# A fused attention and feed-forward kernel: another written-out order of its TensorE groups and loads, and other constants in its planner

## The chip, the core and the metric

One core of a Trainium2 chip. The metric is the device time of one execution in microseconds (us); six executions of the kernel before are at hand. Five engines work side by side, each on its own list of instructions, and wait for one another by semaphores: TensorE (PE, matmuls; PEld is its weight load), VectorE (DVE), ScalarE (ACT), GpSimd (POOL) and SyncE (SP), which here only issues transfers.

## The reference

Attention with a window of 128 tokens and 4 sink tokens for 4 batches of 8 heads, 768 tokens, head size 64; its output, as 3072 tokens of 512 numbers, goes through a feed-forward layer with 2048 hidden units:

```python
scores = (q @ k.T) / sqrt(64);  keep = is_sink | (0 <= rel < 128)
a = exp(scores - max) * keep;   a = a / sum(a);   x = a @ v        # per head
h = x @ w_in;   g = h / (1 + exp(-beta * h));   out = g @ w_out
```

## The kernel before, in words

The tokens are cut into 8 half-batches of 384 tokens ("blocks" 0 to 7, `hb` in the code); each has 4 units of two heads. For a block the kernel loads q, k and v in fp32 (`load`, L613), casts them to bf16 (`cast`, L659), transposes q and k, computes scores, exponentials, masks, the product with v, normalises, transposes the result into `xT`, and then makes the hidden layer and the output. PE's work comes in groups, one letter each:

- T (L690): transposes q and k of a unit on PE, blocks 0 and 1 only; the copy out of PSUM (`qkT<-P`) is DVE's or ACT's. From block 2 on a transfer does it (`XT`, L730, issued by SP: `qkT<-q`, `qkT<-k`).
- S (L812): scores against the sinks; C and D (L764): two groups of window scores (L783), each followed by an exponential on ACT (`E<-P`) and masks on POOL or DVE (L798, L803, L809).
- A (L841): the product with v (L851, L861); then DVE's reciprocal and `onorm` (L868). `vS`, the sinks' rows of v, is copied by DVE (L686) from block v0.
- X (L873): transposes `onorm` into `xT` on PE, blocks 0 and 1; from block 2 on transfers do it (`XO`, L888, two for each block).
- h and g, or H (L899): the hidden layer for 128 hidden units, four matmuls of 128x384 (L910); h is the first two, g the other two. Then tanh on ACT (`t`, L915) and one fused operation on DVE that gives `g` (L917). There are 16 of them in a block.
- O (L925): a quarter of an output tile, four matmuls of 128x512 (L931); after four quarters the tile is copied to `osb` (three buffers, DVE or ACT) and stored by SP (L940).
- b: beta's transpose.

The weights come in sixteen chunks of 512 KB (w0 to w7 for w_in, w8 to w15 for w_out; `load_w`, L640), each cast by DVE, ACT or POOL (`cast_w`, L650) before use. Six staging buffers exist, three of which are borrowed from `g`.

What sets the order:

- `ORDER` (L24) is a string of these letters, found by a search outside of the kernel: PE's groups in the order in which they are issued.
- `PAR` (L23) holds the order of the loads: `l0` permutes the 11 loads of block 0 (indices 0 to 7 are q0, k0, q1, k1, q2, k2, q3, k3 in pairs of heads, 8 to 10 are v0 to v2); `mix` then interleaves the attention loads of blocks 1 and 2 (a) with the weight chunks (w). Both make the list LOADS (L962), which is chained, so that SP issues loads in that order.
- The planner `Graph.schedule` (L148) walks ORDER with a small model of each engine's time (`place`, L106: durations, latencies LAT and HOP, a model of the transfers in flight) and gives every other operation to an engine and a place in its list, the earliest that the model allows. An operation with several possible engines goes to the one that the model has done first. The model runs while the program is built; on the chip only the lists and their semaphore waits remain.
- `fillers` (L301): wherever the model sees PE idle before 48 us, it puts matmuls on the constant tile `ones` (L1027) into PE's list. They are issued in order like any others; nothing reads their result.

SP's list is one queue: loads, stores and transposing transfers are issued in its order, and each that must wait holds all behind it.

Of the kernel before, what the change touches and what calls it, by code (L numbers as in the profile page):

```python
# [21 lines left out]

PAR = {'MD': 1, 'XB': 2, 'l0': [0, 2, 6, 1, 3, 4, 9, 5, 7, 10, 8], 'mix': 'aawwaawawawwawwaaaawwawwawwwawaa'}  # L23
ORDER = ('TCDTSTTDCSDSCASCTADACbXXAhhhXXThghDghgDhggThgggChhgghgShDSghSghghTghgCASCAXADOXOAhhhhXOXOgOOggOOhghg'  # L24
         'hhgOOOghgghghhhghgOgOSDgSChCOghSgADODCCOODOOSAAOAOSSOCCSOSODCHHHHHHHHOHDDOHAHDCHHAHHHAAOODDOOOODCDOH'
         'SCCHHOOASSHHOHOHHHHHSHHHAACSHSOHDCCOAODDOOCCDOAOOHHSHSAOHHOHAAHHHHHHHSHOHOHOSSOCDOHDCCOHHAOOHHHHHSHH'
         'HOSOCCDOHHOHODDAHOAHAOODCCASOOOCDDHHHHHHOAOHOOSHHOOSAHHAOHHHHHOOOHHHHOOHHHHHHOOHHHHOHOOOOOHOOOOOOOOO'
         'OOOOO')
# [9 lines left out]
class Op:  # L38
    __slots__ = ("eng", "fn", "deps", "signal", "count", "waits", "sem", "vc", "dma", "seq", "end", "ns", "alts",
                 "group", "tail", "preds", "left", "succ", "at", "queue", "ring", "lag", "x", "tag", "chain")  # L40

# [5 lines left out]
class Graph:  # L47
# [3 lines left out]
    LAND = {"act": 22, "dve": 23, "gp": 58, "pe": 50, "sp": 26}  # L51
    LEAD, PAD, LATE = 1500, 2000, 90000
    BIAS, EARLY = 300, 100000
    FILL_TO = 48000
    RING, FETCH, SWITCH = 165, 900, 85
    DEPTH = 9

    def __init__(self):
        self.ops = []
        self.groups = []  # L60
        self.writers = {}
        self.readers = {}
        self.last_load = None
        self.filler = None

# [6 lines left out]
    def add(self, eng, fn, ns=0, r=(), w=(), x=(), dma=None, alts=None, queue=470, ring=64, lag=0, after=(), tag=None):  # L72


        o = Op()
        o.eng, o.fn, o.dma, o.ns, o.alts = eng, fn, dma, ns, alts or {eng: (fn, ns)}
        o.queue, o.ring, o.lag, o.x, o.tag, o.chain = queue, ring, lag, list(x), tag, None
        o.signal, o.count, o.waits, o.vc = False, 0, [], None
        o.group, o.seq = None, -1
        if eng == "pe":  # L80
            o.group = self.groups[-1]
            o.group.ops.append(o)
        deps = []
        for k in r:
            ws = self.writers.get(k)
            assert ws, k
            deps += [(p, True) for p in ws]
        for k in w:
            deps += [(p, False) for p in self.readers.get(k, ())]
            deps += [(p, False) for p in self.writers.get(k, ())]  # L90
        for bs, i in x:
            if eng != "pe":
                deps += [(p, False) for p in bs.users[i] if p.eng == "pe"][-1:]
            bs.users[i].append(o)
            bs.left[i] += 1
        deps += [(p, False) for p in after]
        o.deps = deps
        for k in r:
            self.readers.setdefault(k, []).append(o)
        for k in w:  # L100
            self.writers[k] = [o]
            self.readers[k] = []
        self.ops.append(o)
        return o

    def place(self, o, at):  # L106
        o.at = at
        if o.dma:
            self.pending = [x for x in self.pending if x[0] > at]
            issued, need = at + o.queue + 40, min(o.ring, self.RING)  # L110
            total = sum(n for _, n in self.pending)
            for f, n in self.pending:
                if total + need <= self.RING:
                    break
                issued, total = max(issued, f), total - n
            begin = issued + o.lag if o.lag else at + 1150 + o.ns
            self.dma_free = max(self.dma_free + o.ns, begin)
            self.pending.append((self.dma_free, o.ring))
            self.free[o.eng] = issued
            o.end = self.dma_free + 950 + (self.PAD if at > self.LATE else 0)  # L120
        else:
            if o.eng == "pe":
                self.n_pe += 2
                if self.n_pe >= self.fetched + 256:
                    self.fetched += 256
                    self.dma_free = max(self.dma_free, at) + self.FETCH
                rows = o.group is not None and o.group.tag in "CD"
                if rows != self.rows:
                    at = o.at = at + self.SWITCH
                    self.rows = rows  # L130
            self.free[o.eng] = at + o.ns
            o.end = at + o.ns + self.LAT[o.eng]

# [14 lines left out]
    def schedule(self, order):  # L148
# [46 lines left out]
        self.free = {e: 800.0 for e in self.ENGINES}  # L195
        self.dma_free, self.pending, self.n_pe, self.rows, self.fetched = 0.0, [], 0, False, 0
        new = []
# [39 lines left out]
        while at_pe < len(todo) or pool:  # L237
# [20 lines left out]
            for o in pool:  # L258
                opts = []
                for e, (fn, ns) in o.alts.items():  # L260
                    t = self.free[e]
                    for p in o.preds:
                        s = self.seen(p, e)
                        if s > t:
                            t = s
                    if o.dma:
                        t = max(t, self.dma_free - self.LEAD)
                    opts.append((t + ns + (self.BIAS if e == "act" and t < self.EARLY else 0), t, e))
                _, t, e = min(opts)
                by_eng.setdefault(e, []).append((t, o))  # L270
# [7 lines left out]
            if e == "pe":  # L278
                at_pe += 1
                self.fillers(t, banks, holder, new)  # L280
                for bs in fresh.values():
# [18 lines left out]

    def fillers(self, t, banks, holder, new):  # L301

        while self.free["pe"] < min(t, self.FILL_TO):
            slow = 2 if self.free["pe"] < 4900 else 1
# [3 lines left out]
            free = [j for j in range(8) if holder[j] is None and banks[j][0] <= now]  # L308
            n = min(512, int((t - now) * 2.4 / slow) // 128 * 128)
            if not free or n < 128:  # L310
# [4 lines left out]
            o.signal, o.count, o.waits, o.vc, o.chain = False, 0, [], None, None  # L315
            o.deps = [(p, True) for p in self.writers["ones"]] + [(p, False) for p in banks[j][1]]
            o.seq = len(new)
# [137 lines left out]
def _program(nc, G, sb, ps, q, k, v, w_in, w_out, beta, out):  # L455
# [274 lines left out]
    def XT(hb, i):  # L730
# [4 lines left out]
            qkT_all[:, hb % (NT // 4), i, cs[0] * 512:cs[0] * 512 + w].rearrange("p (b t) -> p b t", t=128),  # L735
            x16[n][hb % NX][:, cs[0]:cs[0] + len(cs), :, :].rearrange("p c h d -> p (c h d)")), 1500,
            r=[(n + "16", hb % NX, j, c_) for j in range(4) for c_ in cs],
            w=[("qkT", hb % (NT // 4), j, i, c_) for j in range(4) for c_ in cs], dma=f"dx{n}{hb % 2}", queue=1540, ring=999, lag=1350)

# [24 lines left out]
    def SC(u):  # L764
# [23 lines left out]
        for j, grp in enumerate(gs):  # L788
# [5 lines left out]
            for kind_, sg in (("d", 1), ("p", -1)):  # L794
                at_ = [i for i, blk in enumerate(grp) if blk[0] == kind_]
                if at_:
# [5 lines left out]
                    if UNITS[u][0] < PAR.get('MD', 2):  # L802
                        alts["dve"] = (lambda e, d=d, mk=mk: e.tensor_tensor(d, d, mk, ALU.mult),  # L803
                                       70 + 256 * len(at_) / 1.9)
                    any_of(alts, r=[("E", z, j), ("maskT", int(kind_ == "p"))], w=[(kind_, z, j)])
            if grp[0][0] == "s":
                d = E[z][:, s0:s0 + 2, :, :]
                mask = maskS[:, :, :].unsqueeze(2).to_broadcast([128, 2, 2, 128])
                fn = lambda e, d=d, mask=mask: e.tensor_tensor(d, d, mask, ALU.mult)  # L809
                any_of({"gp": (fn, 1150), "dve": (fn, 335)}, r=[("E", z, j), "maskS"], w=[("s", z, j)])  # L810

# [29 lines left out]
    def AV(u):  # L841
# [5 lines left out]
        for m, ps in enumerate(parts(u)):  # L847
# [8 lines left out]
            for hh in range(2):  # L856
                o0 = (2 * m + hh) * (D + 1)
                for n, (kind_, j, i, kb) in enumerate(ps):
                    vz = (hb if kb >= NK * half else hb - 1) % NV
                    add("pe", lambda e, o0=o0, hh=hh, i=i, kb=kb, vz=vz, a=(n == 0 and not far), o=(n == len(ps) - 1):  # L860
                        e.matmul(A()[:, o0:o0 + D + 1], E[z][:, i, hh, :], vaug[vz][:, kb % NK, 2 * hp + hh, :],  # L861
                                 start=a, stop=o, skip_group_check=True), 39,
                        r=[(kind_, z, j), ("v", vz, kb % NK)], x=[(bs, 0)])
# [24 lines left out]
    def XO(u):  # L888
# [5 lines left out]
            r=[("on", on), ("on", on + 1)], w=[("xT", hp, tl), ("xT", hp + 1, tl)], dma=f"dy{on}", queue=1260,  # L894
            ring=60, lag=700)

# [28 lines left out]
    def OQ(T_, t, j, a=0, b=NOUT):  # L925
# [9 lines left out]
        if j == 3:  # L935
            z = os_i[0] % NOS
            os_i[0] += 1
            any_of(copies(osb[z][:, a:b], lambda: P[:, bk[0], a:b], {"dve": dve_ns(b - a), "act": act_ns(b - a)}, 0.5), w=[("osb", z)],
                   x=[(bk, 0)])
            add("sp", lambda e: e.dma_start(out_t[NK * hb + t][:, a:b], osb[z][:, a:b]), 640 * (b - a) // NOUT, r=[("osb", z)],  # L940
                dma=f"do{z}", queue=370, ring=8)
# [83 lines left out]
    for x, y in zip(LOADS, LOADS[1:]):  # L1025
        loads[y].chain = loads[x]
    G.filler = lambda j, n: lambda e: e.matmul(  # L1027
        P[:, j, 0:n].rearrange("p (a b) -> p a b", b=128), ones[:, :],
        ones[:, :].unsqueeze(1).to_broadcast([128, n // 128, 128]), start=True, stop=True)

# [32 lines left out]
```

The softmax here doesn't subtract the row's maximum and nothing guards it: scores larger than these inputs give would overflow.

## Time and profile before

| | |
|---|---|
| median of 6 runs | 226.93 us (226.66 to 227.8) |
| profiled execution | 226.66 us, span 224.9 us, granted clock 1.0 |
| instructions | 4463 |
| HBM read, written | 27.30 MB, 6.29 MB |
| transfer queue of the loads and stores | busy 79.1% of 16 engines' span |

The page shows busy time for each engine, then the span in 40 slices of 5.6 us (each digit tenths of a slice):

```
PE   8888999999999999999999999999999999999994
DVE  1898999778757277839774578657362626455100
ACT  2595998144882867547788847778756756566221
DMA  7999999996999989999999999994133033101112
```

DMA is the mean busy share of 16 transfer engines; transfers fill the first 28 slices (157 us) and are rare afterwards. In an answer of the trace, a row reads: start, length, engine, line, operation, output <- input, count, and in brackets the idle time just before it and what ended it. In the timeline "x13" is a merged run of 13 instructions. A matmul's own length (326 ns for 128x384) contains its pipeline; the distance from start to start is what it costs in a stream. Landing times of single transfers are "us from issue to landing" in the transfer view.

### The profile page before, as it was taken

How to read it: one execution, taken by the hardware profiler on the slowest of the kernel's cores; microseconds unless marked ns; L12 is line 12 of the kernel's file. 1: busy time of each engine (PE TensorE's matmuls, PEld its weight loads, DVE VectorE, ACT ScalarE, POOL GpSimd, SP SyncE). 2: the span in 40 equal slices, each digit the busy share in tenths (PEclk: the TensorE clock that was granted, in tenths of full speed). 3: DMA queues.
4: the chain of work that ended last, by engine and by line, in shares of the span. 5: the costliest groups of instructions: out<-in, count | busy, mean ns of one | idle time of the engine just before them, and what ended most of it. 6: DMA issues, size and time to landing. Idle time of an engine off the chain costs nothing.

```text
span 224.9 us, 4463 instructions
## 1 busy us (share of the span) xinstructions
PE 215.9 (96%) x1699; PEld 119.4 (53%) x1720; DVE 140.8 (63%) x313; ACT 141.7 (63%) x257; POOL 67.2 (30%) x157
## 2 busy tenths in 40 slices
PE   8888999999999999999999999999999999999994
PEld 2545555555445546545554665555455556555443
DVE  1898999778757277839774578657362626455100
ACT  2595998144882867547788847778756756566221
POOL 8274345000362617352108510241435400000000
PEclk9999999999999999999999999999999999999999
DMA  7999999996999989999999999994133033101112
GB/s 156 267 343 373 356 237 333 346 233 132 215 193 237 218 181 234 196 257 223 205 237 191 199 227 226 252 244 108 47 85 82 0 85 82 47 4 47 47 47 93
DMA packets 104741, 40.95 MB, mean 182 GB/s; under 512 B 93312, under 2 KB 97680, under 8 KB 104720
## 3 DMA queue, kind: packets, MB, share of 16 engines
q1 hardware_dynamic: 103152, 40.65, 79.1%
q8 instruction: 13, 0.21, 0.4%
q10 hardware_dynamic: 1568, 0.02, 0.4%
q14 instruction: 8, 0.07, 0.1%
HBM read 27.30 MB, written 6.29 MB: 149 GB/s over the span
## 4 chain that ended last, share of the span: by engine, by line
PE 69%; DVE 11%; SPq 8%; DMA 7%; ACT 3%; issue 1%
PE P L931 31%; PE P L910 28%; SPq L635 7%; DMA v_stage<-in_v_dram 5%; DVE g L917 4%; PE P L861 4%; PE P L783 3%; DMA out_dram<-osb 2%; PE P L851 1%; DVE onorm L868 1%; ACT t L915 1%; SPq L891 1%; PE P L819 1%; DVE E L803 1%; DVE w_in L563 1%
## 5 line engine op out<-in xcount | busy, mean ns | idle before, releaser
L910 PE MATMUL P<-xT,w_in 128*128 128x384 bf16 x512 | 92.7, 326 | 0.0
L915 ACT ACTIVATE t<-P,hbeta 128x384 f32<-128x384 f32 x128 | 72.0, 587 | 31.0 <-PE P L910 25.2
L931 PE MATMUL P<-w_out,g 128*128 128x512 bf16 (+2 forms) x379 | 89.1, 370 | 1.5 <-ACT t L915 0.2
L917 DVE SCALAR_TENSOR_TENSOR g<-t,P 128x384 bf16<-128x384 f32 x128 | 68.0, 549 | 35.3 <-ACT t L915 32.8
L798 POOL TENSOR_SCALAR_AFFINE_SELECT E<-E 128x256 bf16<-128x256 bf16 (+1 forms) x109 | 53.0, 519 | 57.6 <-ACT E L792 57.6
L910 PEld LDWEIGHTS P<-xT,w_in 128*128 128x128 bf16 x512 | 48.4, 98 | 34.7 <-issue 0.8
L931 PEld LDWEIGHTS P<-w_out,g 128*128 128x128 bf16 x400 | 36.6, 98 | 37.2 <-DVE g L917 1.2
L792 ACT ACTIVATE E<-P 128x768 bf16<-128x768 f32 (+1 forms) x64 | 45.6, 760 | 14.3 <-PE P L783 14.1
L861 PE MATMUL P<-vaug,E 128*128 128x65 bf16 x352 | 18.6, 193 | 0.3 <-DVE vaug L563 0.2
L558 ACT ACTIVATE osb<-P 128x512 f32<-128x512 f32 (+2 forms) x16 | 9.1, 570 | 15.5 <-PE P L931 15.4
L861 PEld LDWEIGHTS P<-vaug,E 128*128 128x128 bf16 x352 | 16.5, 97 | 3.6 <-ACT E L792 0.7
L868 DVE TENSOR_TENSOR onorm<-P,rden 128x384 bf16<-128x384 f32 x32 | 17.5, 553 | 0.5
L783 PE MATMUL P<-qkT 64*128 64x128 bf16 (+1 forms) x256 | 16.6, 239 | 1.2 <-DMA qkT<-k 0.5
L823 ACT ACTIVATE ES<-P 128x128 bf16<-128x128 f32 (+1 forms) x32 | 12.1, 391 | 7.0 <-PE P L819 7.0
L563 DVE CAST k<-k_stage 128x512 bf16<-128x512 f32 (+1 forms) x24 | 11.2, 466 | 6.3 <-DMA k_stage<-in_k_dram 6.1
L783 PEld LDWEIGHTS P<-qkT 64*128 64x128 bf16 x256 | 8.3, 94 | 12.5 <-issue 3.6
L563 DVE CAST q<-q_stage 128x512 bf16<-128x512 f32 (+1 forms) x19 | 8.8, 465 | 7.3 <-DMA q_stage<-in_q_dram 7.2
L851 PE MATMUL P<-vS,ES 128*128 128x130 bf16 x64 | 12.7, 221 | 0.6 <-DVE vS L686 0.4
L563 DVE CAST vaug<-v_stage 128x512 bf16<-128x512 f32 x18 | 7.9, 441 | 7.8 <-DMA v_stage<-in_v_dram 7.7
L725 POOL TENSOR_TENSOR kS<-qkT,headm 128x8 bf16<-128x8 bf16 x16 | 3.0, 211 | 32.4 <-DMA qkT<-k 29.0
L1027 PE MATMUL P<-ones 128*128 128x512 bf16 (+2 forms) x31 | 9.9, 446 | 1.2 <-POOL ones L569 1.1
L809 DVE TENSOR_TENSOR E<-E,maskS 128x512 bf16<-128x512 bf16 x16 | 7.9, 495 | 3.5 <-ACT E L792 3.4
(48 smaller groups left out, 88.8 us busy)
## 6 DMA issues: line engine op xcount, KB each, us to landing
v_stage<-in_v_dram SPq DMA_DIRECT2D x24, 256.0 KB, 4.5
out_dram<-osb SPq DMA_DIRECT2D x23, 256.0 KB, 2.5
q_stage<-in_q_dram SPq DMA_DIRECT2D x18, 256.0 KB, 4.7
k_stage<-in_k_dram SPq DMA_DIRECT2D x18, 256.0 KB, 5.8
wst<-in_moe_w_in_dram SPq DMA_DIRECT2D x5, 512.0 KB, 6.4
wst<-in_moe_w_out_dram SPq DMA_DIRECT2D x4, 512.0 KB, 7.7
g<-in_moe_w_out_dram SPq DMA_DIRECT2D x4, 512.0 KB, 7.7
q_stage<-in_q_dram SPq DMA_DIRECT2D x8, 192.0 KB, 4.6
```

The source lines that it names most:

```text
L563: return lambda e: e.tensor_copy(dst, at())
L635: o = add("sp", lambda e: e.dma_start(dst, src), ns, w=[("stg", n, z, j) for j in keys], dma=f"d{n}{z}{'' if i is None else i}", ring={610 ...
L783: add("pe", lambda e, dst=dst, own=own, kc=kc, rows=rows, q0=q0, nq=nq: e.matmul(dst(), tokens(own, hp, 1, rows, kc, 1)[:, 0, :], tokens(h ...
L792: add("act", lambda e, src=src, dst_=dst_: e.activation(dst_, src(), AF.Exp, bias=0.0, scale=SCALE), act_ns(256 * n), w=[(k_, z, j) for k_ ...
L798: alts = {"gp": (lambda e, d=d, sg=sg, at_=at_: e.affine_select(d, d, [[0, 2 * len(at_)], [sg, 128]], ALU.is_ge, 0.0, base=min(sg, 0), cha ...
L851: add("pe", lambda e, m=m, o0=o0: e.matmul(A()[:, o0:o0 + 2 * (D + 1)], ES[z][:, (c0 + m) * 128:(c0 + m + 1) * 128], vS[b % 2][:, 2 * hp:2 ...
L861: e.matmul(A()[:, o0:o0 + D + 1], E[z][:, i, hh, :], vaug[vz][:, kb % NK, 2 * hp + hh, :], start=a, stop=o, skip_group_check=True), 39,
L868: add("dve", lambda e: e.tensor_tensor(onorm[:, on, 2 * c0:2 * c1, :], av()[:, :, 0:D], rden[on][:, 0:2 * nb].unsqueeze(2).to_broadcast([1 ...
L910: first = add("pe", lambda e, c=c: e.matmul(hp(), w_in16[:, c, m * 128:(m + 1) * 128], xT[:, hb, c, 128 * c0:128 * c1], start=(c == 0), st ...
L915: add("act", lambda e: e.activation(tt[ti][:, 0:n], hp(), AF.Tanh, bias=0.0, scale=hbeta[:, m:m + 1]), act_ns(n) + 93, r=["hbeta"], w=[("t ...
L917: add("dve", lambda e: e.scalar_tensor_tensor(gt[hb % NG][:, m, 128 * c0:128 * c1], tt[ti][:, 0:n], 1.0, hp(), ALU.add, ALU.mult), dve_ns( ...
L931: add("pe", lambda e, m=m: e.matmul(P[:, bk[0], a:b], gt[hb % NG][:, m, t * 128:(t + 1) * 128], w_out16[:, m, a:b], start=(m == 0), stop=( ...
```

## The change

PE's order, the order of the loads, and the constants of the planner's model. No operation of the computation is added or removed. The core of the diff:

```diff
-PAR = {'MD': 1, 'XB': 2, 'l0': [0, 2, 6, 1, 3, 4, 9, 5, 7, 10, 8], 'mix': 'aawwaawawawwawwaaaawwawwawwwawaa'}
-ORDER = ('TCDTSTTDCSDSCASCTADACbXXAhhhXXThghDghgDhggThgggChhgghgShDSghSghghTghgCASCAXADOXOAhhhhXOXOgOOggOOhghg'
+PAR = {'MD': 1, 'XB': 2, 'l0': [0, 1, 9, 3, 2, 4, 6, 5, 7, 10, 8], 'mix': 'aawwaawwwaawwaawaaawwwwwwwaaaawa'}
+ORDER = ('TTTSCDCTCSDSTACSDAbDXCAXDAhhhXhXTghhghgghgggghThhCggDSghghhTSghghCgSDSgAACDXAXOhOAOXOXOhgOhghgghOOhh'
...
-    LEAD, PAD, LATE = 1500, 2000, 90000
-    BIAS, EARLY = 300, 100000
+    LEAD, PAD, LATE = 2000, 2000, 90000
+    BIAS, EARLY = 400, 100000
...
-    RING, FETCH, SWITCH = 165, 900, 85
-    DEPTH = 9
+    FETCH, SHORT, SWITCH = 1150, 400, 85
+    DMA = {"nat": ((434, 580, 580, 580, 470), 64, 1140, 115, 2250), "hb": ((434, 580, 580, 580, 470), 64, 2290, 115, 3390),
...
+    DEPTH = 8
+    FETCHES = (152, 232, 368, 477, 608, 730, 858, 988, 1111, 1222, 1354, 1482, 1601, 1728)
...
-            total = sum(n for _, n in self.pending)
-            for f, n in self.pending:
-                if total + need <= self.RING:
...
+            wait, total = at, sum(x[2] for x in self.pending)
+            for b, f, m, _ in self.pending:
+                if total <= room:
+                    break
...
-                    if o.dma:
+                    if o.dma and e == "sp":
                         t = max(t, self.dma_free - self.LEAD)
...
-                self.fillers(t, banks, holder, new)
+                self.fillers(t, g.tag in "CD", banks, holder, new)
...
-                                       70 + 256 * len(at_) / 1.9)
+                                       150 + 256 * len(at_) / 1.6)
...
-                any_of({"gp": (fn, 1150), "dve": (fn, 335)}, r=[("E", z, j), "maskS"], w=[("s", z, j)])
+                any_of({"gp": (fn, 1150), "dve": (fn, 430)}, r=[("E", z, j), "maskS"], w=[("s", z, j)])
...
-            add("sp", lambda e: e.dma_start(out_t[NK * hb + t][:, a:b], osb[z][:, a:b]), 640 * (b - a) // NOUT, r=[("osb", z)],
+            add(PAR.get('OUT', "sp"), lambda e: e.dma_start(out_t[NK * hb + t][:, a:b], osb[z][:, a:b]), 640 * (b - a) // NOUT, r=[("osb", z)],
```

`PAR` has no entry OUT, so stores stay on SP.

What the new lists hold, counted engine by engine in the two built programs: PE 1726 instructions instead of 1722; the difference is fillers (26 of 512 columns, 4 of 384 and 1 of 256 become 31 of 512, and a few smaller). DVE has 320 instead of 315, ACT 256 instead of 261, POOL 161 and SP 144 in both. Two qkT copies and one w_in cast go from ACT to DVE, two k casts and a few others to POOL. The first groups of PE's list are now T T T S C D C T instead of T C D T S T T D; 9 fillers instead of 12 stand ahead of the first T, 12 between the first two, 6 and a half ahead of the third. The first loads are q0, k0, v1, k1, q1, q2, q3, k2, k3, v2, v0 instead of q0, q1, q3, k0, k1, q2, v1, k2, k3, v2, v0. In SP's list the first store (L940) now stands ahead of the q and k loads of block 3 instead of behind them, and the transposing transfer of block 3's k stands behind both xT transfers of block 2 (L891 before) and a store instead of ahead of them; the v loads of block 3 follow.

## Prediction

> **What bounds the kernel now.** I read the page's busy times first, then the chain that ended last.
>
> ```profile
> PE 215.9 (96%) x1699; PEld 119.4 (53%) x1720; DVE 140.8 (63%) x313; ACT 141.7 (63%) x257; POOL 67.2 (30%) x157
> ...
> PE 69%; DVE 11%; SPq 8%; DMA 7%; ACT 3%; issue 1%
> ```
>
> TensorE is the bound, but 96% hides something: "busy" includes the fillers (L1027, matmuls on `ones` whose result nobody reads). So I counted the wanted matmuls and priced each shape by the distance between starts in the PE timeline where nothing waits: 216 ns for 128x512 (20 of L931 from 208.25 to 212.56), 163 for 128x384 (L910), 57 for 128x128, 30 for 128x65 (L861), 58 for 128x130 (L851), 45 to 85 for the half-row scores (L783). The sum is 204.0 us. PE runs from 1.06 to its end at 222.05, so 18.05 us of these 222 are not wanted work. An order can change only that. Where does it lie? Cut the trace at five landmarks and put the wanted work beside each stretch:
>
> ```profile
> 0.00:21.18 21.18, 17.93 (x168) 9.80 (x169) 14.69 (x36) 11.82 (x22) 12.46 (x40) 1.00 1.02 279
> 21.18:38.08 16.90, 16.17 (x156) 9.14 (x154) 15.85 (x34) 15.97 (x30) 7.13 (x13) 1.00 1.03 314
> 38.08:57.07 18.99, 18.89 (x119) 10.40 (x121) 15.88 (x36) 7.60 (x15) 1.33 (x3) 1.00 0.96 240
> 57.07:84.69 27.62, 26.41 (x209) 13.36 (x211) 17.00 (x39) 18.82 (x36) 11.82 (x28) 1.00 1.04 209
> 84.69:222.05 137.36, 136.47 (x1055) 76.69 (x1068) 77.38 (x173) 87.25 (x157) 34.44 (x75) 1.00 0.68 139
> ```
>
> Columns: length, then busy time of PE, PEld, DVE, ACT, POOL, granted clock, DMA share, GB/s. Wanted PE work in the five is 7.45, 14.39, 19.05, 25.58 and 137.53 us, so lost are 13.73 (start-up), 2.51, -0.06, 2.04 and -0.17. The last stretch loses nothing. In the second, DVE is busy 15.85 of 16.90 us and ACT 15.97: both are full. The fourth is neither; its losses are single waits:
>
> ```profile
> 73.30 0.51 PE L783 MATMUL P<-qkT 64*128 64x256 bf16 x8 [0.47 <-DMA qkT<-k]
> ...
> 76.33 5.38 PE L910 MATMUL P<-xT,w_in 128*128 128x384 bf16 x32
> 81.76 1.32 PE L931 MATMUL P<-w_out,g 128*128 128x512 bf16 x3
> ...
> 84.42 0.34 PE L783 MATMUL P<-qkT 64*128 64x256 bf16 x3 [0.32 <-DVE g L917]
> ```
>
> Three L931 matmuls at 81.76 take 1.16 us to the next start instead of 0.65, and 84.42 waits again, both behind DVE, which was itself held by transfers:
>
> ```profile
> 74.02 0.69 DVE L564 TENSOR_SCALAR osb<-P 128x512 f32<-128x512 f32 x1 [1.88 <-DMA out_dram<-osb]
> 77.00 0.69 DVE L564 TENSOR_SCALAR osb<-P 128x512 f32<-128x512 f32 x1 [2.29 <-DMA out_dram<-osb]
> 78.91 0.47 DVE L563 CAST vaug<-v_stage 128x512 bf16<-128x512 f32 x1 [1.22 <-DMA v_stage<-in_v_dram]
> ...
> 81.28 0.43 DVE L563 CAST vaug<-v_stage 128x512 bf16<-128x512 f32 x1 [0.97 <-DMA v_stage<-in_v_dram]
> ```
>
> **The change, part by part.** Wanted matmuls are the same, 204.0 us. The constants of the planner put no instruction into the kernel; what moves is the order on five engines and the fillers: 31 with 15,104 columns become 36 with about 17,000. A filler costs only where it runs past the data that it waits for.
>
> *Start-up.* The new load order brings q0 and k0 first. Before, q0 was cast at 3.71, the second load at 4.78 and k0, the fourth, at 6.23, and PE waited 0.59 us for it (transposes at 6.72). Now transposes can start after k0's cast, about 4.8+0.4 = 5.2. But the second and third transposes come later than before: q1 is now the fifth load (6.87 by the old fifth), the next 12 fillers run to 5.3+0.34+12x0.216 = 8.2, then six and a half more to 9.9. And v0, the block on which the first attention waits (chain: DMA to 12.26), is the 11th load in both orders, with the same bytes ahead: nothing gained there. I walked DVE's new list with the old durations (cast 0.34, qkT copy 0.87, mask 0.32, rden 0.1, onorm 0.47, xT 0.27, w_in 0.60): four qkT copies now sit on DVE before v0 (two before the change) in time in which DVE idled; v0's cast 12.6 to 12.9; the sinks' copies end at 14.6 (before: 13.7); the four onorms end at 16.2, 17.1, 19.5, 20.2 (before: 16.6, 17.8, 18.8, 20.0); the last xT copy 20.5 to 20.8. ACT's eight exponentials start later (10.2 instead of 8.7) but have one qkT copy between instead of three, 2 x 0.7 us less, and end near 16.6 as before. So the dense run of L910 starts at about 21.2 as before, but with 8.04 us of wanted work behind it instead of 7.45: lost 13.2 instead of 13.7. **Gain 0.5**; bounds -0.5 (the walk is no better than half a microsecond) to 1.2.
>
> [...] The trace: fillers start 424 ns apart up to 4.45 ((4.45-1.06)/8), then about 215.
>
> ```profile
> 4.02 1.06 PE L1027 MATMUL P<-ones 128*128 128x512 bf16 x2
> 4.45 1.14 PE L1027 MATMUL P<-ones 128*128 128x512 bf16 x3
> ```
>
> So the array was released 3.4 us after its first matmul (the granted clock column reads 1.00 even there and does not show it). [...]
>
> *Second stretch.* DVE decides. From the first g (about 23.1) to the second w_out cast, on which the first L931 waits, the new list holds 14 g (0.465), 6 weight casts, 4 q/k casts, a qkT copy, 3 v casts, 2 onorm, 2 rden: 14.5 us, so about 37.6, if no load is late. Weights w3 and w4 now come ahead of a q/k pair, v and the first two w_out chunks have the same bytes ahead as before (landing 34.1 and 35.5 by issue plus time to landing, their casts at 35.9 and 37.0). First L931 at 37.7 with 22.0 us of wanted work done, against 38.08 with 21.84: lost 15.7 instead of 16.24; no further gain or loss here (bounds -0.5 to +0.5). The third stretch loses nothing before; the second pair of w_out casts is due at 41.3 by PE and done at 40.2: zero.
>
> *Fourth stretch.* Here the changed queue counts. First scores of block 3 (the wait at 73.30) stand 4.6 us of wanted work later in the PE order. In SP's queue their transposing transfer now stands behind both xT transfers of block 2: q transfer 66.2, xT 67.8, store 69.1, xT 69.9 (its onorm, behind k casts that land at 66.97, 68.05, 68.95, ends 69.8), k transfer 71.2, landing about 75.5. The scores are due at 60.5+15.7 = 76.2: covered by 0.7, the 0.47 goes. The first L910 of block 2 is due at 57.9+15.7 = 73.6 and its xT lands 3.3 us after 69.9, at 73.2 to 73.6: no cover, 0 to 0.5 late. The first store moves ahead of six q/k loads (57.9 instead of 65.77), so DVE's evictions do not wait as at 74.02 and 77.00; v follows at 73.5 instead of 75.04, and its casts stand after four g's instead of after none, so the g's behind the waits at 78.91 and 81.28 run first. Of 2.04 lost I leave 0.9: **gain 1.1**, bounds -1.0 (the xT transfer late) to 2.0.
>
> *Last stretch.* Nothing was lost, so nothing can be gained; I looked for pairs that come closer. From the last attention of a block to the first L910 of the block that reads it, wanted work between is 6.6 to 9.9 us for blocks 3 to 7 (before 7.0 to 12), more than the 5.6 that onorm, issue (1.3) and landing (3.3) need: zero, bounds -0.3 to +0.8. The end is the same run of L931 and the same last 128-column store.
>
> Sum against the profiled run (226.66, span 224.9): 226.66 - 0.5 - 1.1 = 225.1. Its time lies 0.27 below the median of the six, so 225.3; as every new order brings some waits that a walk does not find, I say 225.4.
>
> **The rivals.** *Nothing moves* (226.4): v0 and DVE bound the first 38 us in both orders, and a new wait in the fourth stretch eats what the old ones give. For it: v0's place is unchanged. Against: two of the three waits lose their cause. *Slower* (227.9): the xT transfer at place 42 of SP's queue waits for the last onorm of block 2, now behind two k casts on DVE; k transfer, store, v loads and the next q/k loads stand behind it. If k of block 3 lands at 72 instead of 69, all shift by 3 us and PE, with no cover at its first L910 of block 2, stands for it: 225.1+3 = 228.1, less some overlap. It decides once that k lands 1.7 us late. For it: DMA share is 1.04 there. Against: before, the same bytes landed in time, with the same loads ahead. *More* (224.3): the dense run starts 0.7 earlier too.
>
> **How the numbers follow.** Forecast 0.50, more 0.08, nothing moves 0.22, slower 0.20. A measurement tells 0.3% (0.7 us) from no change: faster below 226.25. Range 224.3 to 227.6: the lower bound of the forecast and most of the slower case; about 0.15 left out.
>
> **What would show it.** Right: the first L931 near 37.7; no PE wait on qkT<-k near 73 to 77; the first store issued near 58; no DVE wait on out_dram of 2 us; PE's end near 220.4. Wrong: first L910 of block 2 waiting on xT; the third transposes after 10.5; exponentials of block 0 ending after 17.5; any PE wait over 0.5 us after 85.

## The result, and the profile after

The changed kernel takes 229.93 us (median of 17 runs) against 226.93 for the kernel before (38 runs): ratio 1.0113, 95% interval 1.0094 to 1.0132, so 3.0 us **slower** in the medians. The ratio leaves out four slow executions of the changed kernel (one of 1249.25 us and three at 231 us), so by it the difference is 2.6 us. The forecast was 225.4, and the measured time lies outside its range. The one profiled execution that came with this result was a freak (1249.25 us; its matmuls of 384 columns start 1.05 us apart in the median, before's 0.163), so the changed kernel was profiled again twice, and everything below is read from those two profiles (called again, 228.78 us, and again2, 229.50 us). Lines of the changed kernel are those of before plus 41 in the helpers: L910 is L951, L931 is L972, L564 is L605.

From the page of again, the busy times, and the granted clock in 40 slices of 5.7 us:

```profile
PE 218.6 (96%) x1724; PEld 120.7 (53%) x1724; DVE 144.6 (64%) x318; ACT 138.6 (61%) x252; POOL 68.4 (30%) x157
...
PEclk9997999999999999999999999999999999999999
```

TensorE is still at 96%. New is the 7 in the clock row: in the fourth slice (17 to 23 us) the array did not have its full clock; from 15 to 20 us the granted clock was 0.66, which makes 3.4 us at half clock. The trace's record of the clock begins with the release of the array (its change to full clock) at 5.99 us in again and at 5.10 in before: before's fillers of 512 columns start 427 ns apart up to 4.88 and 216 from 5.21 on, and in again the transposes at 5.33 still take 0.50 us, those at 8.40 0.33. Cut from there into stretches of 3.41 us, the length of the time at half clock, the second, third and fourth are, again first (columns: length, busy time of PE, PEld, DVE, ACT, POOL, granted clock, DMA share, GB/s):

```profile
9.40:12.81 3.41, 3.06 (x39) 1.79 (x37) 3.33 (x7) 2.12 (x5) 1.30 (x3) 1.00 1.26 254
12.81:16.22 3.41, 2.12 (x30) 1.32 (x31) 3.36 (x11) 2.90 (x7) 2.85 (x8) 1.00 0.94 324
16.22:19.64 3.42, 3.42 (x36) 2.15 (x37) 2.30 (x8) 2.92 (x6) 2.79 (x5) 0.50 1.05 376
```

and before:

```profile
8.51:11.92 3.41, 3.37 (x45) 1.96 (x39) 2.98 (x6) 3.09 (x6) 1.77 (x6) 1.00 1.28 251
11.92:15.34 3.42, 2.47 (x38) 1.58 (x38) 3.04 (x9) 3.29 (x7) 2.79 (x7) 1.00 1.07 356
15.34:18.75 3.41, 2.97 (x43) 1.90 (x39) 3.41 (x9) 3.14 (x7) 2.68 (x4) 1.00 1.08 369
```

In again TensorE was busy 2.12 of 3.41 us, and for the next 3.42 us it got half the clock (0.50) while it had work all the time. Before was busy 2.47 of 3.42 us in its third stretch and kept its clock. (The expectation of fill_four below counts stretches that lie 0.13 us earlier: 2.00 of 3.42 us.) TensorE's timeline of again shows the hole and the landmarks that the prediction spoke of:

```profile
14.21 0.34 PE L738 MATMUL P<-ident,q 128*128 128x128 bf16 x3 [1.10 <-ACT E L833]
...
23.12 4.43 PE L951 MATMUL P<-xT,w_in 128*128 128x384 bf16 x26
...
39.85 1.23 PE L972 MATMUL P<-w_out,g 128*128 128x512 bf16 x4
...
76.21 2.76 PE L951 MATMUL P<-xT,w_in 128*128 128x384 bf16 x16
79.09 0.51 PE L824 MATMUL P<-qkT 64*128 64x256 bf16 x8
...
81.64 2.12 PE L951 MATMUL P<-xT,w_in 128*128 128x384 bf16 x12 [1.29 <-DVE osb L605]
```

With the forecast's own measure (start time less wanted work done): lost 15.08 us at the dense run (23.12, wanted 8.04), 17.84 at the first w_out group (39.85, wanted 22.01), 18.36 at 76.21, 20.04 at 85.61, 20.17 at PE's end (224.17). Before lost 13.73, 16.24, then 18.22 at 84.69 and 18.05 at the end. So of the 2.1 us by which again is behind, 1.35 are there when the dense run starts. In again2 the dense run starts at 24.52: lost 16.48, because there the array had half its clock for two such stretches, 15.83 to 22.66 (granted clock 0.58 from 15 to 20 us, 0.73 from 20 to 25). TensorE had work throughout the first of them (busy 4.96 of the 5 us from 15 to 20); why a second one follows in most executions and not in all stayed open.

Behind the two bracketed waits stand these rows of VectorE and, first, of ScalarE:

```profile
11.71 2.49 ACT L833 ACTIVATE E<-P 128x512 bf16<-128x512 f32 x4
...
13.54 0.62 DVE L604 CAST q<-q_stage 128x384 bf16<-128x384 f32 x1
...
80.89 0.69 DVE L605 TENSOR_SCALAR osb<-P 128x512 f32<-128x512 f32 x1 [2.02 <-DMA out_dram<-osb]
```

The cast of block 1's q ends at 14.16, the fourth exponential, which the row names, at 14.20, and the transposes start at 14.21. The two end within 0.04 us of each other, so no run shows that either alone is the cause. VectorE ran without a gap from 10.7 us on. The eviction at 80.89 waits for a store. SP's queue says why:

```profile
58.30 0.64 SPq L983 DMA_DIRECT2D out_dram<-osb  x1
...
72.97 0.58 SPq L983 DMA_DIRECT2D out_dram<-osb  x1
73.59 1.25 SPq L932 DMA_TRANSPOSE xT<-onorm  x1
74.88 1.52 SPq L775 DMA_TRANSPOSE qkT<-k  x1
76.44 0.90 SPq L983 DMA_DIRECT2D out_dram<-osb  x1
```

The first store went out at 58.30 as forecast. The second and third, whose evictions were done at 58.14 and 61.74, went out at 72.97 and 76.44 only: six loads and four transposing transfers stood before the third.

### The profile page after: what moved, and what is told of

Read it like the earlier page. It is cut to its first block, busy times and chain, and to the rows that moved or that the text cites. A ratio compares the mean times of both kernels' runs of the same rounds, so it can differ in the third digit from the quotient of the medians.

```text
span 1247.5 us, 4471 instructions
## 1 busy us (share of the span) xinstructions
PE 1222.0 (98%) x1701; PEld 421.0 (34%) x1724; DVE 146.7 (12%) x318; ACT 148.7 (12%) x252; POOL 65.9 (5%) x157
## 4 chain that ended last, share of the span: by engine, by line
PE 98%; issue 2%; ACT 0%; POOL 0%; POOLq 0%
PE P L951 41%; PE P L972 39%; PE P L902 5%; PE P L824 5%; PE P L1070 4%; PE P L892 2%; PE P L860 2%; PE P L738 1%; PE P L921 1%; ACT E L833 0%; ACT t L956 0%; ACT ES L864 0%; ACT osb L599 0%; PE P L643 0%; POOL ones L610 0%
## 5 line engine op out<-in xcount | busy, mean ns | idle before, releaser
L951 PE MATMUL P<-xT,w_in 128*128 128x384 bf16 x512 | 525.4, 1369 | 1.9 <-issue 1.9
L972 PE MATMUL P<-w_out,g 128*128 128x512 bf16 (+2 forms) x377 | 497.7, 1640 | 19.7 <-issue 16.9
L951 PEld LDWEIGHTS P<-xT,w_in 128*128 128x128 bf16 x512 | 157.6, 311 | 335.0 <-issue 331.2
L972 PEld LDWEIGHTS P<-w_out,g 128*128 128x128 bf16 x400 | 121.1, 308 | 312.4 <-issue 308.6
L839 POOL TENSOR_SCALAR_AFFINE_SELECT E<-E 128x512 bf16<-128x512 bf16 (+1 forms) x108 | 51.2, 499 | 756.8 <-ACT E L833 756.6
L902 PEld LDWEIGHTS P<-vaug,E 128*128 128x128 bf16 x352 | 74.9, 258 | 32.0 <-issue 28.6
L902 PE MATMUL P<-vaug,E 128*128 128x65 bf16 x352 | 85.4, 484 | 0.0
L824 PE MATMUL P<-qkT 64*128 64x128 bf16 (+1 forms) x256 | 61.1, 747 | 0.0
L1070 PE MATMUL P<-ones 128*128 128x512 bf16 (+3 forms) x35 | 46.2, 1618 | 1.1 <-POOL ones L610 1.1
L860 PE MATMUL P<-qkT,kS 128*128 128x128 bf16 (+1 forms) x32 | 28.9, 968 | 0.0
```

The source lines that it names most:

```text
L824: add("pe", lambda e, dst=dst, own=own, kc=kc, rows=rows, q0=q0, nq=nq: e.matmul(dst(), tokens(own, hp, 1, rows, kc, 1)[:, 0, :], tokens(h ...
L839: alts = {"gp": (lambda e, d=d, sg=sg, at_=at_: e.affine_select(d, d, [[0, 2 * len(at_)], [sg, 128]], ALU.is_ge, 0.0, base=min(sg, 0), cha ...
L860: add("pe", lambda e: e.matmul(P[:, bs[0], q0:q1].rearrange("p (s w) -> p s w", w=128), kS[hp][:, :], tokens(hb, hp, 0, slice(0, 128), q0, ...
L951: first = add("pe", lambda e, c=c: e.matmul(hp(), w_in16[:, c, m * 128:(m + 1) * 128], xT[:, hb, c, 128 * c0:128 * c1], start=(c == 0), st ...
L972: add("pe", lambda e, m=m: e.matmul(P[:, bk[0], a:b], gt[hb % NG][:, m, t * 128:(t + 1) * 128], w_out16[:, m, a:b], start=(m == 0), stop=( ...
L1070: G.filler = lambda j, n: lambda e: e.matmul(P[:, j, 0:n].rearrange("p (a b) -> p a b", b=128), ones[:, :], ones[:, :].unsqueeze(1).to_bro ...
```

## The experiments

Two theories for the 3 us, and their rivals. **Clock**: the hole at 13.1 to 14.2 us makes the array fall to half clock for one or two stretches of 3.4 us (rival: the new order is slow by itself and the clock only goes along). **Stores**: the second and third store sit too late in SP's queue (rival: something else is late next, so moving them gains nothing). "Re-planned" below means that the planner ran again with the edit and moved operations on all engines; "frozen" means that every list was left as the planner had made it and only the named entries were touched, after `G.schedule(ORDER)` (the four fillers while PE's list is written out). The edits are shown shortened. Where fillers (matmuls on `ones`) are added or dropped, no result changes.

**again, again2**: the changed kernel unchanged.

> The changed kernel itself, for a trace of an ordinary execution. Its first profiled execution ran every matmul six times too slowly (span 1247.5 us), its other runs list a mean granted clock of 0.985 where all of before list 1.000. Theory A (clock gate): a stretch of half clock stands somewhere in the trace; 0.985 of 228 us is 3.4 us lost, which is the whole difference of 3.0 us; outside of it the new order loses no more than before (16 to 18 us of unwanted PE time), and matmuls there start 427 ns apart for 512 columns instead of 216. Theory B (waits): no such stretch; the 3 us are PE waits in the stretch from 57 to 85 us (xT of block 2, qkT of block 3) or after it. Time near 229.9 by both.

> The changed kernel once more, for a trace of an execution with mean clock 0.985 (the last trace caught one with 0.992: one half-clock stretch of 3.4 us, 16.1 to 19.5). Theory A: two such stretches, adjoining, beginning 3.4 us times a whole number after the release of the array at the start; the dense run of L951 starts 1.5 to 2.5 us later than the 23.12 of the last trace, and the time after it is equal. Theory B: the second stretch lies where PE has slack, and the extra 2 us stand as waits after 40 us.

Measured 229.93 us (228.78 to 231.52), ratio 1.0116 (1.0066 to 1.0166), and 229.50. In the 22 other runs of the changed kernel the mean clock was .992 (3 runs, mean 228.2 us) or .983 to .985 (19 runs, mean 230.1 us). One stretch of 3.4 us at half clock takes 1.7/222 = .008 off the mean, two take .015, so these are one and two such stretches, and with the second an execution is about 1.9 us longer (three runs against 19). Before has .998 to 1.000 or, in about one run of three, .992, with no difference in time to speak of (227.1 us in the mean of 22 runs of one comparison, 227.2 in that of its 13 others).

**order_only, planner_only** (re-planned): the two halves of the change.

```diff
-PAR, ORDER of before            # order_only: before's planner, new PAR and ORDER
+PAR, ORDER of after
-PAR, ORDER of after             # planner_only: after's planner, old PAR and ORDER
+PAR, ORDER of before
```

> New order of groups and loads, planner constants of before (8 fillers instead of 9 ahead of the first transposes, 9 instead of 12 ahead of the second, one less later on). Theory A: fewer fillers early, so the array's activity is lower or its phase other; if the half-clock stretch comes from the first 20 us of the new order it is here too: about 229.5 to 231, clock near 0.985. Theory B: the waits come from the order of SP's and DVE's lists, which this planner makes otherwise; between 226.5 and 231, clock 1.000.

> Order of groups and loads of before, planner constants of after (17 fillers instead of 12 ahead of the first transposes). Theory A: the sparse start of the new order is gone, PE is fuller at the start than before: clock 1.000 and 226.5 to 229. Theory B: the planner's lists carry the loss: 228.5 or more at clock 1.000.

232.98 us, ratio 1.0251 (1.0223 to 1.0278), clock .985 in every run, and 232.33, ratio 1.0213 (1.0185 to 1.0240), clock .992 to 1.000. Each half alone is slower than both together, so the halves don't add. In the first every run had two slow stretches; in the second the loss lies elsewhere, since its run at 1.000 took as long as those at .992. As a split of the 3 us this pair tells nothing.

**keep_busy, thin** (re-planned): fillers forced ahead of each group between 10.3 and 14.5 us of model time in the new kernel; no fillers after 8 us in the old one.

```diff
+                if 10300 < self.free["pe"] < 14500:          # keep_busy
+                    t = max(t, self.free["pe"] + 230)
-    FILL_TO = 48000                                          # thin
+    FILL_TO = 8000
```

> The changed kernel with extra fillers ahead of the groups between 10 and 14.5 us (about 11 of 128 to 512 columns, some 1.2 us of PE, where it waits for exponentials). Theory A: the window before 15 us is no longer sparse, the array stays at full clock; clock 0.992 or 1.000 in most runs and a time of 227.0 to 228.7, 1 to 3 us less than the changed kernel, in spite of the added work. Theory B: clock may rise, the time does not fall: 229.5 to 231.

> The kernel before without any filler after 8 us (ten fillers fewer). Theory A: activity between 8 and 20 us falls under what the gate asks for, half clock for one or two windows in every run, clock 0.985 to 0.992; time 228 to 230.5. Theory B: fillers are of no use once the array is released: 226.5 to 227.5.

keep_busy: clock .999 to 1.000 in all runs, yet 231.44 us, ratio 1.0226 (1.0164 to 1.0289). thin: clock .978 to .993, 229.83 us, ratio 1.0101 (1.0072 to 1.0129), though its profiled run, at .992, was no slower than before (span 225.6). Both fit the theory that fillers decide the clock; neither shows what the clock costs, because the planner had re-made all lists. From here on lists were frozen.

**fill_four** (frozen): four fillers in the hole.

```diff
+    # ahead of the fifth T group, into the bank that is free there
+    4 x matmul(P[:, 3, 0:512], ones, ones)
```

> The kernel after with every engine's list left as it is, and only four matmuls of 512 columns on the constant tile put into TensorE's list ahead of the fifth group of transposes (the wait of 1.10 us at 14.21). Clock theory: that wait is the sparse stretch (TensorE busy 2.00 of the 3.42 us from 12.67 to 16.09) for which the next 3.4 us were granted half the clock; four fillers are 0.86 us and lie inside the wait, so the stretch is busy 2.9 of 3.42 as in the kernel before, the clock row stays 1.00 from 16 to 20 us, the mean clock is .992 or more, the dense run of x26 begins near 21.7 in place of 23.1 or 24.5, and the median falls from 229.9 to 226.5 to 227.8. Order theory (the new group order itself costs the time at start-up, the clock only goes along with it): the clock may return, but the dense run still begins after 23 and the time stays within 229.2 to 230.5.

```profile
12.83 1.04 PE L1080 MATMUL P<-ones 128*128 128x512 bf16 x4
13.99 0.34 PE L748 MATMUL P<-ident,q 128*128 128x128 bf16 x3
...
22.45 4.43 PE L961 MATMUL P<-xT,w_in 128*128 128x384 bf16 x26
...
77.59 2.45 PE L961 MATMUL P<-xT,w_in 128*128 128x384 bf16 x14 [1.56 <-DMA xT<-onorm]
```

(TensorE's timeline; lines are shifted by ten.) The clock was 1.000 in all six runs: with the hole filled the clock did not fall. Time 228.88 us, ratio 1.0093 (1.0071 to 1.0115): 1.05 us better than the changed kernel, half of the gain expected by the clock theory and more than the order theory allowed. The last row shows where the other half went. From the fifth transposes to the dense run is now 8.46 us; it was 8.91 in again (one slow stretch) and 10.38 in again2 (two), so the slow clock cost 0.45 and 1.9 us there. But PE then comes to block 2 earlier than its second xT transfer and stands 1.56 us at the third matmul, where again had stood 1.29 for the eviction: fill_four's PE ends at 224.18, again's at 224.17, again2's at 224.89. So in these traces one slow stretch costs nothing in the end: fill_four's mean (228.9) is no lower than that of the three executions with one stretch (228.2), only lower than that of the 19 with two (230.1).

**drop_five** (frozen): the kernel before without its fillers between 10 and 20 us.

```diff
+    G.ops = [o for o in G.ops if not (filler(o) and 10000 < o.at < 20000)]
```

> The kernel before with every engine's list left as it is, and only the fillers that its planner put between 10 and 20 us of its own time taken out of TensorE's list (about nine matmuls, 1.6 us of work that computes nothing). Clock theory: TensorE is then busy about 2.3 of the 3.4 us around 11 to 14.5 and the array falls to half clock for one or two stretches of 3.4 us after it; the mean clock is .992 to .985, the first dense runs begin 1 to 2.5 us later than before's, and the time rises to 228 to 230. Order theory: fillers only fill waits, so the time is within 0.4 us of before's 226.9, or a little lower.

```profile
10.73:14.14 3.41, 2.35 (x35) 1.26 (x35) 2.90 (x7) 3.25 (x7) 2.86 (x8) 1.00 1.14 304
14.14:17.55 3.41, 3.41 (x42) 2.42 (x41) 3.41 (x13) 2.70 (x7) 2.31 (x5) 0.50 1.05 369
```

(The third and fourth stretch from its release at 3.90.) The clock fell as expected (.991 to .993 in 18 of 22 runs, .985 in one), the time did not follow: 227.00 us, ratio 1.0001 (0.9984 to 1.0018). A clear miss of the clock theory as I had put it. TensorE works 3.41 of 3.41 us at half clock and still has the first w_out group at 37.73, not later than before's 38.08. But the edit also took work away: between 14.14 and 20.97 us before was idle for 0.6 us and spent 1.27 us on fillers, and one stretch at half clock can cost 1.7 us at most (an estimate: half of its 3.41 us). So this pair shows that fall and fillers came out even here; what the fall alone costs it does not show. drop_five's dense run even waits 0.48 us for VectorE's `xT` at 21.33.

**stores_early** (frozen), **fill_and_stores** (frozen): the second and third store directly behind the last load of k; alone, and with the four fillers.

```diff
 SP: ... k_stage x3,
+    out_dram<-osb x2,
     qkT<-q, xT<-onorm,
-    out_dram<-osb,
     xT<-onorm, qkT<-k,
-    out_dram<-osb,
     v_stage x3 ...
```

> The kernel after with only two entries of the load queue moved: the second and third stores of the result (issued at 72.97 and 76.44, though their copies were done at 58.1 and 61.7) stand ahead of the transposing transfers, directly behind the last load of k near 67.1. Store theory: VectorE's wait of 2.02 us on the third store at 80.89 and TensorE's wait of 1.29 us at 81.64 go, TensorE has lost about 1.3 us less at 85.6 than in the run of after, and the median falls by 0.9 to 1.5 us, to 228.4 to 229.0. Rival: what is late next takes its place (the transposing transfers of q, xT and k are each pushed back by two stores' issue of 0.6 us, or the scores' exps end late), and the time stays within 0.4 us of 229.9.

> Both edits together: four fillers ahead of the fifth group of transposes, and the second and third stores ahead of the transposing transfers. If both theories hold the gains add: 2.1 to 3.4 from the clock and 0.9 to 1.5 from the stores, a median of 225.2 to 226.8, below before's 226.9. If only the clock theory holds it equals the run with the fillers alone; if only the store theory holds, the run with the stores alone.

SP's queue and then TensorE's timeline of stores_early:

```profile
68.25 1.45 SPq L993 DMA_DIRECT2D out_dram<-osb  x2
71.65 1.42 SPq L785 DMA_TRANSPOSE qkT<-q  x1
```

```profile
78.00 2.76 PE L961 MATMUL P<-xT,w_in 128*128 128x384 bf16 x16
80.70 0.50 PE L834 MATMUL P<-qkT 64*128 64x256 bf16 x8
81.13 2.77 PE L961 MATMUL P<-xT,w_in 128*128 128x384 bf16 x16
```

The bracket of 1.29 is gone and nothing came in its place there. 228.81 us, ratio 1.0085 (1.0062 to 1.0108): 1.1 us better than the changed kernel, as the store theory said. With both edits 227.69 us, ratio 1.0044 (1.0026 to 1.0061), 2.2 us better than the changed kernel: the two gains add (1.05 and 1.1, and 1.1 and 1.2 when the other edit is already in; stores_early has two slow stretches in all its runs, as 19 of the 22 of the changed kernel have, and fill_four and fill_and_stores have none), but the sum stays 0.8 us behind before and misses the 226.8 that I had given as the upper end. Starts of the same instructions of the changed kernel, in us:

| | fifth T | dense run | second w_out group | w_out group near 88 | PE's end |
|---|---|---|---|---|---|
| again | 14.21 | 23.12 | 41.25 | 88.85 | 224.17 |
| again2 | 14.14 | 24.52 | 42.65 | 89.07 | 224.89 |
| fill_four | 13.99 | 22.45 | 40.57 | 88.26 | 224.18 |
| stores_early | 14.37 | 24.92 | 43.04 | 88.99 | 225.38 |
| fill_and_stores | 13.95 | 22.41 | 40.54 | 87.14 | 223.29 |

Between the third and the fourth column the stores give 1.09 us where no stretch was slow (47.69 in fill_four, 46.60 in fill_and_stores), but only 0.47 where two were (46.42 in again2, 45.95 in stores_early). In again2 TensorE's own wait for the eviction is 0.30 us, not 1.29; so the 1.1 us of the medians is shown by the times, and where it lies in such an execution is in part open. From the fourth column to the end again needs 135.3 us and again2 135.8, but fill_and_stores 136.2 and stores_early 136.4. One wait is named in each of the last two, on a late xT and, behind a VectorE cast that had waited 1.70 us for a load of v, on g:

```profile
123.66 1.15 PE L971 MATMUL P<-xT,w_in 128*128 128x384 bf16 x6 [0.66 <-DMA xT<-onorm]
```

```profile
158.27 1.47 PE L961 MATMUL P<-xT,w_in 128*128 128x384 bf16 x8 [0.90 <-DVE g L968]
```

**cast_on_act** (frozen): fill_and_stores with one weight cast of 0.68 us moved from VectorE to ScalarE's idle time. **before_stores** (frozen): the store edit in the kernel before.

```diff
+    c.eng = "act"; c.fn, c.ns = c.alts["act"]      # w_in cast at 21.81
```

```diff
 SP: ... out_dram<-osb,                             # before_stores
+    out_dram<-osb x2,
     qkT<-q, qkT<-k,
-    out_dram<-osb,
     xT<-onorm x2,
-    out_dram<-osb,
     v_stage x3 ...
```

> The run with both edits (fillers and stores, 227.69 us) with one more entry moved and no list otherwise changed: one cast of 1024 weights (0.68 us at 21.81 on VectorE) is done by ScalarE, which is idle from 20.68 to 22.06 there. VectorE theory for the 0.8 us that is left over before: VectorE runs without a gap from 19.4 to 39 us with 37.9 us of work before the first w_out group against 34.3 in before, so its list sets when the first w_out group starts (39.4 against 38.1); 0.68 us less of it brings that group to 38.7 to 38.9 and the median to 226.9 to 227.3. Rival: the score exps on ScalarE and the transposes on TensorE set it, and the first w_out group stays at 39.2 to 39.4 and the median at 227.5 to 227.9.

> The kernel before with only two entries of the load queue moved: its second and third stores of the result (issued at 70.87 and 74.42, copies done at 53.9 and 58.5) directly behind the first at 65.77. Store theory: VectorE's waits of 0.22, 1.88 and 2.29 us on out_dram at 69.6, 74.0 and 77.0 go; TensorE's named waits in that stretch are only 0.47 (transposed k) and 0.32 (g), so it gains 0.3 to 0.9 us and the median falls to 226.0 to 226.6. Rival: TensorE does not follow VectorE there, and the time is within 0.2 us of 226.9; or the pushed transposing transfers cost 0.3.

VectorE in cast_on_act, and TensorE in before_stores:

```profile
23.00 0.96 DVE L628 COPY qkT<-P 128x768 bf16<-128x768 bf16 x1 [0.51 <-PE P L762]
```

```profile
72.15 0.50 PE L825 MATMUL P<-qkT,kS 128*128 128x384 bf16 x2 [0.63 <-DMA qkT<-q]
73.84 0.51 PE L789 MATMUL P<-qkT 64*128 64x256 bf16 x8 [0.33 <-DMA qkT<-k]
```

cast_on_act: 227.52 us, ratio 1.0020 (1.0005 to 1.0034), 0.17 from fill_and_stores, within their scatter. The time that VectorE was given it spent waiting (0.51) for the transposes that come next in PE's list; from the dense run (23.01) to the second w_out group (41.13) it is 18.12 us, as in fill_and_stores (18.13), and from the fifth transposes (14.54) to the dense run 8.47, there 8.46. The first w_out group (39.74) falls in neither expected range, because this execution's fifth transposes were 0.6 us later. So this cast does not set the start-up; the median is in the rival's range.

before_stores: 226.94 us, ratio 0.9990 (0.9966 to 1.0015). VectorE's waits on stores of 1.88 and 2.29 us are gone, and the time is the same: the pushed transposing transfers are late instead. So in the kernel before, VectorE's waits on stores did not cost TensorE time; in the changed kernel they did.

**stores_on_act** (re-planned): the stores issued by ScalarE's queue, the evictions on ScalarE.

```diff
-PAR = {'MD': 1, 'XB': 2, ...
+PAR = {'MD': 1, 'XB': 2, 'OUT': 'act', ...
```

> The changed kernel with stores issued by ACT instead of SP; PE's list is the same instruction for instruction. It tests the PE wait of 1.29 us at 81.64, behind a DVE eviction that waits for the third store, itself behind two transposing transfers in SP's queue. If that wait is a part of the loss: it is gone, 228.2 to 229.0. If ACT's own list pays for the issues (0.5 to 0.9 us each on SP), 229.5 to 231. The clock does not change: 0.985.

235.65 us, ratio 1.0379 (1.0333 to 1.0424). All lists had been re-made, so this run does not tell what another queue for the stores is worth; moving them within frozen lists does. None of the versions tried is faster than before.

## Why the prediction was wrong

**Start-up, "gain 0.5".** Forecast: dense run at 21.2, lost 13.2. Measured: 15.08 (again) and 16.48 (again2). Two terms failed.

The first is the walk of VectorE's list. It had the transposes of block 1 start without a wait, the exponentials of block 0 end "near 16.6 as before" and the last onorm at 20.2. Even at full clock (fill_and_stores) the exponentials end at 17.8 (past 17.5, the prediction's own sign of being wrong) and the last onorm at 21.6, and the dense run has lost 14.4: 1.2 us more than forecast. The walk saw that four copies of `qkT` now sit on VectorE and called the time before v0 idle; it was full (4.91 of 5 us busy from 10 to 15), and TensorE stood 1.10 us until the q cast at its end and ScalarE's fourth exponential were done. It also priced each mask operation at 0.32 us, while one of them takes 1.12 us at 15.34 in fill_and_stores, as one did in the profile of before (1.13 at 15.03), which was there to be read.

The second was not in the sum at all: the clock. The prediction speaks of it only for the time at which the array is *first* released. That did move: from 5.10 in before's profile to 5.99 in again, whose first transposes (at 4.98 and 5.33) still take the cold 0.5 us; in fill_four those at 4.44 already take 0.34, in cast_on_act those at 5.40 still 0.50. (The prediction read 4.45 for before; but the fillers at 4.45 and 4.88 still start 0.43 us apart, so the release came some 4.0 us after the first matmul, not 3.4.) But what cost time was the fall back afterwards. Ahead of it the longest gap in again was 1.10 us, and TensorE had been busy for 2.12 of 3.41 us. That the hole is the trigger in this kernel is shown by fill_four (clock 1.000 in six of six runs); what it costs is 0.45 us for one slow stretch and 1.9 for two at the dense run, and 1.05 us in the median.

**Second stretch, "no further gain or loss".** Lost 2.76 in again and 2.75 in fill_four (its first w_out group at 39.17, by the shift of 0.68 of the next one); the forecast had 2.5. Right within its bounds. Its place was wrong (first w_out group 39.85, not 37.7) only through the start-up.

**Fourth stretch, "gain 1.1".** Of its parts these came: the first store at 58.30, no wait on the transposed k at 79.09, no wait on xT at 76.21. The failing step is "The first store moves ahead ... so DVE's evictions do not wait": it followed one store and not the next two, which stood in the same queue behind everything else. stores_early shows that this step alone was worth 1.1 us in the median. And the waits on stores were no cost in the kernel before: before_stores removes those at 74.02 and 77.00, and its time is the same, so the gain could not have come from them. With it mended (fill_and_stores) TensorE loses 1.2 us between the first w_out group and 84 us against 1.98 before: 0.8 gained, where the forecast had 1.1.

**Last stretch, "nothing can be gained".** 0.13 lost in again: right. In fill_and_stores, which arrives earlier, TensorE loses about 1.0, of which 0.66 is the wait on xT at 123.66. The distances between attention and the layer that reads it had been checked at the old arrival times only. So with both repairs the kernel is still 2.3 us over the forecast of 225.4, mostly the 1.2 of the walk and the 1.0 here.

**The rivals.** "Slower" ended on the right side and by the wrong mechanism: no xT transfer was late in again. It was second in line, though: as soon as the clock was mended (fill_four) the first hidden group of block 2 did wait for xT, 1.56 us at its third matmul, the sign that the prediction had named.

What stays open: the 0.8 us by which fill_and_stores is behind before. In the profiles it is 0.9 us at the first w_out group (lost 17.1 against 16.24), -0.8 in the fourth stretch and +1.1 in the last. cast_on_act rules out one cast as cause of the first; which link of the chain from loads through VectorE, transposes and exponentials sets it was not found. Nor was it settled what made re-planned lists lose 2 to 4 us.

## What to carry to other kernels

A hole in TensorE's work can be paid twice: in again 1.10 us as a wait, and 0.45 us more at the dense run by the 3.4 us at half clock that came after it. So set TensorE's busy time and the granted clock side by side, stretch by stretch, in a trace that kept its clock and in one that did not (here before kept it with 2.47 of 3.42 us busy; drop_five lost it after 2.35 of 3.41, again after 2.12), and try fillers in the hole, but first ask whether the slow stretch after it has idle time to pay with. When a store moves forward in a queue, follow every store that shares its buffers, not the first. And change frozen lists when testing a planned kernel: an edit that re-runs the planner tests a different kernel.

## What the runs showed of the hardware

- Seven profiles show the array at half clock for 3.4 to 3.5 us, or for 6.9 (order_only, again2), of the time from 10 to 25 us. TensorE's busy time from 10 to 15 us and, in brackets, the granted clock from 10 to 15, 15 to 20 and 20 to 25: order_only 3.24 (.91, .50, .90), again2 3.35 (1.00, .58, .73), again 3.40 (1.00, .66, 1.00), stores_on_act 3.46 (1.00, .73, .93), thin 3.54 (1.00, .66, 1.00), planner_only 3.70 (.97, .69, 1.00), drop_five 3.92 (.91, .74, 1.00). In before and before_stores (4.01 each), fill_four (4.34), cast_on_act (4.38) and keep_busy (5.00) all three read 1.00; of before's other executions about one in three lists .992.
- From the change to full clock to the fall it was 10.23 us in again (5.99 to 16.22) and 10.24 in drop_five (3.90 to 14.14).
- A hole alone did not bring the fall: drop_five waited 1.15 us ahead of the transposes at 6.69, so that TensorE was busy 2.26 of 3.41 us from 3.90 to 7.31 (1.91 us of it fillers of 512 columns), and its clock stayed at 1.00 from 5 to 10 us and up to 14.14. What decides it stayed open.
- In the cold start the view of the granted clock reads 1.00 although matmuls of 512 columns are 427 ns apart (before, 1.46 to 4.88 us), because the trace's record begins with the release, at 5.10; later falls it does show (0.50 in a stretch of 3.42 us in again).
- One execution in 23 of the changed kernel took 1249.25 us, with 1.05 us from start to start of matmuls of 384 columns (the median) in place of 0.163; its trace has no record of the clock, and the view reads 1.00. It did not come again and its cause is unknown.
